# A kernel whose whole instruction order is a table of 4,801 codes: the table searched anew, with the planner's durations rescaled and its margin behind VectorE's reads cut

## The chip, the cores and the metric

One core of a Trainium2 chip. The metric is device time in microseconds (us) of one execution. TensorE is PE in the profile, its weight loads PEld, VectorE DVE, ScalarE ACT, GpSimd POOL, and the engine that issues the DMAs SP.

## The reference, cut to what matters

Two branches over the same 2048 x 512 input `x`, mixed by a gate per row:

```python
# S=2048, D=512, H=32 heads of 16, one shared K and V, F=1792
g = sigmoid((x * gate_w).sum(-1, keepdims=True))
q = (x @ wq).reshape(B, S, H, Dh).transpose(0, 2, 1, 3)
k, v = x @ wk, x @ wv
p = softmax(einsum("bhqd,bkd->bhqk", q, k) * Dh ** -0.5)
a = einsum("bhqk,bkd->bhqd", p, v).transpose(0, 2, 1, 3).reshape(B, S, H * Dh) @ wo
b = (sigmoid(x @ w_gate) * (x @ w_up)) @ w_down
out = g * a + (1 - g) * b
```

## The kernel before

**Tiling.** The attention is cut into 32 units `u` (4 blocks of 512 queries x 8 groups of 4 heads) with 16 key chunks `c` each. A unit first needs the largest score of each query (`maximum`, "m": a matmul at L1148 into a PSUM bank, then a reduction of that bank by VectorE at L1150, 2048 of each). Then come the scores again with the maximum subtracted ("s": a matmul at L1157, then the exponential by ScalarE at L1159, 2048 of each), and after that the product with V (`values`, "V": four 32-column matmuls at L1015, in two passes each, 512 V's in all; each uses the four exponential tiles of one chunk). The feed-forward branch and the output projection are matmuls at L1122 ("f", 4404 of them) that add up in two PSUM banks held for long.

**Two halves.** m, s and f matmuls contract over 64 rows only, so PE runs two at once, one in each half of its rows. One such pair is called a *pair step* here. V fills the whole array. So PE alternates between *stretches* of pair steps and *runs* of V's.

**Banks.** PSUM has 8 banks. An m or s takes a free bank and gives it back when VectorE (m) or ScalarE (s) has read it. A run of V's adds up in one bank. When the run ends, `finish` copies the bank out by ScalarE (L1022), and unless it is the unit's first copy GpSimd adds it to the others (`add_sums`, L1029). A finished f sum is read by ScalarE (`gate` L1131), by VectorE (`gated` L1137), or by `part_of`: the first part of an output tile by ScalarE (L1098), a later one either by VectorE, which adds it to the tile (L1079, "sum"), or by ScalarE into a spare tile (L1098, "apart") that GpSimd then adds (L1101). `gather` chooses between the last two when the program is built, by which would be done first in the plan.

**What sets the order.** `ORDER` is a string. Each code stands for one step of PE: `V` one V, `G` one of 24 opening matmul groups (keys, queries, transposes), `.` a planned wait of 25 units, and a hex digit a pair step whose two base-4 digits say what each half does (1 m, 2 s, 3 f, 0 nothing; so `7` is m beside f, `b` s beside f, `5` m beside m). `State.step` walks the string, keeps a clock in units for each engine, and decides from it which bank is taken, where the readers, the POOL tasks and the DMAs are placed in their engines' queues, and how a part is added. A pair step is 100 units. The rest of the constants are durations in the same units: `RED` a VectorE reduction, `EXP` an exponential, `VALUES` a V, `IN` and `OUT` the change to V's and back, `LATE` from a matmul's start to its reader's, `TAIL` and `FREE` from a reader's end until PE may take the bank again (`FREE_A` behind ScalarE).

```python
    def issue_m(self, h):
        i = self.take()
        ...
        self.free[i] = self.on("dve", self.now + LATE, RED) + TAIL + FREE
```

On the chip there is no clock: every engine executes its own list in order and waits on semaphores. A `.` emits nothing. So if a bank is free sooner than planned PE goes on, and if it is free later PE waits.

Of the kernel before, what the change touches and what calls it, by code (L numbers as in the profile page):

```python
# [31 lines left out]
OU, VB = 2, 2  # L32
# [13 lines left out]
MAX_SPLIT, SQUARE, SEND_SQUARE, PLACE = 180, 75, 220, 320  # L46
EXP, COPY, SCALED = 208, 210, 247
TAIL, TAIL_A = 38, 52

SEEN = 10  # L50


IN, OUT, VALUES = 52, 106, 371

CAST, TWO, CAST_W, TWO_W = 265, 556, 450, 1030


ISSUE, SMALL, TEN_KB, LAST, SAFE, SURE = 185, 750, 20, 300, 300, 150


BEGIN = 2420, 3500, 3200, 2300, 3500, 5250
X1_THERE, WQ_THERE = 5300, (3200, 3450, 4050, 4050)
LATER = (("load_x", 2), 8000), (("load_x", 3), 8100)
FEED_AT = 12200


TURN_OVER, SEEN_OVER = 40, 100
# [55 lines left out]
class State:  # L123

    def __init__(self):
# [3 lines left out]
        self.free, self.sum = [0] * 7 + [4100], None  # L129
# [12 lines left out]
        self.raws, self.raw_free = [], [4700, 6000]  # L142
# [26 lines left out]
    def send(self, n, kb):  # L169

        self.on("sp", self.now, n * ISSUE)
        self.on("dma", self.sp, kb * TEN_KB // 10)
        return max(self.sp + SMALL, self.dma + LAST)

    def issue(self, cost, kb):

        self.on("sp", self.now, cost)
        self.on("dma", self.sp, kb * TEN_KB // 10)
        return max(self.sp + SMALL, self.dma + LAST)
# [39 lines left out]
    def run(self, t):  # L219
# [8 lines left out]
        at = self.on("pool", t[2] if t[2] >= self.ticked else self.ticked + 50, cost)  # L228
# [17 lines left out]
        elif what == "divide":  # L246
            self.divided(args[0], at)
        elif what == "x":
            self.x_done[args[0]] += 1
            if self.x_done[args[0]] == KC // 2:  # L250
                self.x_ready[args[0]] = at + SURE
        elif what == "xf":
            self.x_there[args[0]] = at
        elif what == "max_split":
            self.after(at + 50, "max_square", *args)
        elif what == "wq":

            self.w_there[args[0]] = at if args[0] else at - 500
        else:
            self.ready[args[0]] = at + SURE  # L260
# [33 lines left out]
    def event(self, what, args):  # L294
# [11 lines left out]
        elif what == "place_max":  # L306
            self.max_ready[args[0]] = self.issue(PLACE, 16) + 150
        elif what == "store":
            at = self.sums_free[args[0] % OU] = self.issue(470, 264) + SAFE
            self.after(at, "sums", *args)  # L310
        elif what == "sums":
            self.after(self.issue(430, 136) + 2 * SAFE, "invert", *args)
# [5 lines left out]
        elif what == "spread":  # L318
            u = args[0]
            at = self.issue(250, 128)  # L320
# [108 lines left out]
    def settle(self):  # L429
        for h in range(2):  # L430
            while self.at[h] is not None:
# [13 lines left out]
                elif j.kind == "u":  # L445
# [3 lines left out]
                    self.task(0, at + 50, "h", slot, j.b, 2 * j.i + x)  # L449
# [63 lines left out]
    def issue_m(self, h):  # L513
# [4 lines left out]
        if self.mp[h] == min(self.mp) and self.mp[h] % (2 * NC) == 0:  # L518
            u = self.mp[h] // (2 * NC) - 1
            self.acts.append(("max_finish", u))  # L520
            self.task(0, self.on("dve", 0, ENDS) + 50, "max_split", u)
# [69 lines left out]
    def issue_g(self):  # L591
# [4 lines left out]
        if what == "turn":  # L596
            self.now += 300
            self.ba_release(("v", b), self.now + LATE)
            at = self.on("dve", self.now + LATE - 100, 250)
            self.acts.append(("turned", b, i))  # L600
        else:
            for _ in range(KC):
                self.now += 300
                self.tick()
            at = self.now + LATE - 100
            self.ba_take((what, b, t), 1)
            if what == "keys":
                self.ba_take(("v", b), 1)
                at = self.on("dve", self.on("act", at, 250) + 50, SUM)
                self.ba_release((what, b, t), at)  # L610
                self.k_ready[b] = at + 100
# [5 lines left out]
        self.done += 300 if what == "turn" else 1200  # L617
# [4 lines left out]
    def split_first(self):  # L622
        b = self.next_x
        if b < NB and self.x_loaded[b] <= self.now and (b < 3 or self.first >= GROUPS.index(("turn", 1, 0))):
# [6 lines left out]
            if b == 1:  # L631
                self.x_there[b] = self.on("dve", at - 600, 4 * RED)
# [49 lines left out]
    "fb7ededeef7b7f9f6fbf6fedf75VV59aV692aVV569VV56effedefbdaf7f6bfdb7b7bbdfdbbfd6fef7f7ddd5VVVV7b7bdbedfe7ef6dbfb7ed"
    "ededbf7bb7f6fedebfdfb5VVVVV7b7b79bffbdafdf6fededeedef7e7fb7e7eedff7b5bV95aVVVVV977bfbdef9fb7e7ebdfedeedef7b77bf9"
    "fef6f9ff5eV595VVVVV7b7b7bbdf9fafde7edfedeede7ff6ef7edb7bfefb7aV995VVV565VV7b7b7bbdfeedfedb7fededee7ef7edef97efb7"
    "bbd7bVVV599VVV7b7bb77bbdfbededfedededeef77eef7edbb7fefb75VVVV9edff6edf6fef97bdbfb7b7bbfd6fdefedef7df7775VVV959VV"
    "97b7fbdefbdeb7f9f6fededeef7b7f9faf7b7deff5dVVVVV7b7edbdbf6f9fb7bfededeedef7e7f6f6fef9fb7fb9VVVV969VV6b7bfde7fed6"
    "fede7efbb77bbdfedfedbdb7eeffb75VV596VV596VV997ffbf6f9fbb7dbefdededee7f6ff6f9f7efbff79aVV955VVVV7b7b7b9ff9fbe7edf"
    "edededee7ff6fb76fedefbfb76VV5a9VVVde5eefb7f9fee7dbfbf7ba77fedfedef9bf7bdff755VVVVVdeded6effb7bf9f6fe7b7bb7bfd9ff"
    "ed6fbdeff75dbVVVV65aV6deedffb7b7b7bdbffdde5VV696Vdede6fbf7b7b7bdefbdfd6VVV9b7fde7bfbdbdbb7fedededeef76ffb7bfa7fd"
    "ff5d5VVVVV7b5bbffedb7ee7bdf6fededeedf7bf6faf7f9fff7aaVVV995VVVdee6fdf6fe7bb7fedfb7b7bbdfbd9fef9f6fe7ffd56VVVV6ed"  # L690
    "ededff6fb7be7fbdb7b7bbfdedfb79febdf6fef5VV665VV995VV6deedf7bfb7eedf6fbdb77bb7efdeedfedbf9bf7fb5V695VV956VV95aVV6"
    "7bff9dbf6fef6eddefb7bb7bdfbd7bf6fedefbfedaV695VV695VVVV7b7b7bf9fbdef6.dbdefedeedef7b7ef6fdef6ff7b5a..7V599VV5aaV"
    "V96aVV6eddfef6f6f9fe7bbfdb77bb7efedfed9fbf9b7fdf5VV569VVVV7b7bb7fededeb7f9fe7edededbf7bfe7bb7edbfdfd5VVVV677bbfd"
    "ef6f9feb7bfdededee7fb7ef79fe7bfffd55VVV659VV7b97bfbfded6fbbdf6feeddee7f7bf6fafdf6fbdf5bVVVVV6deef7dbf6fafd7bedfb"
    "7bb7bfdedf9feb7f6bdfef5VV956VVV97bb7b7ffbdedbe7fededeede7fb7fede7bbdf7f7d5VVVVV97fb7bdefb79fbe7efdededee7fb7dbfe"
    "7bdbf6fefaV955VVVVV6dedefe7f6fb7ebdef7b7bb7bdf9ffbdbde7ebfdfd6V695VVVV7b7b7bbdf9fbedf6fedededee7f7ef6f6febdfb7bf"
    "6V959VVVVV6deedef7fe7bedb7dbfb7bb7bdfedefd6fbdbfff575VVV9a6VV696V6ddeeff9f6f9fe7bfbdb7bb7bdff97bfedb7efedef5VV66"
    "9VV559VVV7b7b7bf9fbdeed7efe7ededeef7b7fedef6f9fb7bf9VV569VV6deeeddffb7bf6deb7fb7bb7bdf9ffe7bdeedff7d57VVVVV977bb"
    "7bffbdbedf9fedeeddee7f6ff6f6fbb7efdf76VVV995VVV5b7b7bfefed9fe7bf9fedededef6ff6fb7bfbdeb77dVVV955VVV7b97fbfededed"
    "efefbb7afdfffe7b7b7bf6fedfe5VVVV6dedefe7fe7bbddbfe7b7bb7bdfbdf6fedbe7bdff5dVV659VVV7b7bb7bdf9febd7efededeede7f7e"  # L700
    "bf7bde7bf7fde9VVV5a6VV59aV7b7b7b7bbfdbdeedfedededeef7e7fe7e7bf9fbdf75VVVVVV5eedef7efe79febdfb7b7b7bbfd9fbdfb7bf6"
    "defeddVV655VVV7b7bb7bdfbde7edbdefededee7fe7fe7b7bbddeff76V9a9VV665VV596VV5bbfdeefde76fbdef9f7bb7bbfddbfb7be7f9ee"
    "fedeV659VV695VV56aVV6ddeef7efedb7ebdb7fb7bb77efedfedbdbb7fedf5bV956VV5aaVV96aVVV97bff9e7f6fbf9f97efededeef7b7f9f"
    "6fb7ff7ddd5VVVV7b7bb77bfedbf9defedededeef7b7fe7b7edeef7bf5VV596VV956VV95effef6fedbedf6fb7b7b7bbfdedfbde7ebdbff7d"
    "5VVVV65aV6ddefbf9fe7ef6f9fbdb7b7bbfd7befdbde7efbdd7dVVVVV67bb7bfdf9fbf6edef7ededeef7b7f9faf7dbfe7efbb777VVVVVV9f"
    "dbbdfbe6fdfedededeef76fbf6fdb7efb7f95VV955VVV7b7b97bffedef6dbf9fededeef77e7bf6fef9bbffd5VVVVV7b7b7bb7fedafdedfbd"
    "ededeef7b7fe7e7ef9f9ff76V595VVVVded6fbf6fede7bf97efb7bb7bdff9fb7edeb7dffdd6VV659VVV5e7bfebdfe7edeb7fedbb7b7bbfdf"
# [559 lines left out]
```

## Time and profile before

| | |
|---|---|
| median of 3 runs | 1564.77 us (1564.64 to 1565.0) |
| profiled execution | 1567.49 us, its span 1564.9 us |
| granted PE clock | 1.00 |
| busy share: PE / DVE / ACT / POOL | 99% / 85% / 78% / 51% |
| span up to the first pair step behind the last opening group | 84.4 us |

Read PE's 99% with care. Pair steps overlap two matmuls, and a matmul's record may begin before its weights are loaded, so waits hide inside "busy". The start-to-start spacing of PE's rows is the better measure.

### The profile page before, as it was taken

The numbers are of one execution on the slowest core, as the hardware profiler recorded it, in microseconds if no ns is written. First come the engines' busy times: TensorE is split into PE (matmuls) and PEld (weight loads), VectorE is DVE, ScalarE is ACT, GpSimd is POOL, SyncE is SP. The second block draws the span as 40 slices with busy tenths as digits, with TensorE's granted clock in tenths as the row PEclk, the third lists the DMA queues.
The fourth block names the chain that finished last, engine by engine and source line by source line (L and its number), as shares of the span: only waits on it lengthen the run. The fifth ranks groups of instructions, "written<-read, shape, count | busy, mean of one in ns | idle before, by whom it ended". The sixth has DMA issues, their size and how long they took to land.

```text
span 1564.9 us, 33526 instructions
## 1 busy us (share of the span) xinstructions
PE 1555.2 (99%) x12910; PEld 983.3 (63%) x12910; DVE 1333.5 (85%) x2278; ACT 1228.4 (78%) x2429; POOL 799.4 (51%) x727
## 2 busy tenths in 40 slices
PE   9999999999999999999999999999999999999998
PEld 7766666666656666666655666666665666665653
DVE  6999899988899788889798888898889888888852
ACT  4267778878788787879788787877878878787897
POOL 3353473655584164377475346265658426438351
PEclk9999999999999999999999999999999999999999
DMA  6522120212122121122221212022212212111011
GB/s 233 179 89 57 36 79 24 67 54 89 43 80 65 46 81 53 33 73 63 61 80 54 76 36 87 17 67 67 77 36 91 63 43 80 53 36 56 23 50 48
DMA packets 63219, 103.42 MB, mean 66 GB/s; under 512 B 24546, under 2 KB 25058, under 8 KB 63060
## 3 DMA queue, kind: packets, MB, share of 16 engines
q1 hardware_dynamic: 63060, 101.29, 20.7%
q8 instruction: 101, 1.65, 0.4%
q14 instruction: 58, 0.48, 0.1%
HBM read 79.51 MB, written 21.75 MB: 65 GB/s over the span
## 4 chain that ended last, share of the span: by engine, by line
PE 95%; POOL 2%; DVE 1%; DMA 1%; issue 0%; SPq 0%; ACT 0%; DVEq 0%; POOLq 0%; ACTq 0%
PE bank L1015 29%; PE bank L1122 27%; PE bank L1157 19%; PE bank L1148 17%; PE bank L860 3%; DVE mx L1150 1%; DMA rg<-wg 0%; POOL ou L1029 0%; POOL wu L835 0%; DMA od<-ou 0%; DMA qs<-md 0%; POOL hl L761 0%; PE bank L1203 0%; POOL wg L835 0%; POOL wu L834 0%
## 5 line engine op out<-in xcount | busy, mean ns | idle before, releaser
L1150 DVE TENSOR_REDUCE mx<-bank 128x1 f32<-128x512 f32 x2048 | 1249.1, 681 | 163.9 <-PE bank L1148 102.0
L1159 ACT ACTIVATE p<-bank 128x512 f32<-128x512 f32 x2048 | 1042.2, 690 | 3.6 <-PE bank L1157 1.8
L1157 PE MATMUL bank<-qs,ks 64*128 64x512 f32 x2048 | 727.2, 400 | 0.1
L1148 PE MATMUL bank<-ks,qs 64*128 64x512 f32 x2048 | 682.2, 401 | 0.0
L1015 PE MATMUL bank<-p,v_aug 128*32 128x512 f32 x4096 | 480.1, 597 | 0.0
L1157 PEld LDWEIGHTS bank<-qs,ks 64*128 64x128 f32 x2048 | 359.1, 184 | 127.2 <-ACT p L1159 52.5
L1148 PEld LDWEIGHTS bank<-ks,qs 64*128 64x128 f32 x2048 | 341.9, 185 | 148.7 <-issue 57.2
L1022 ACT COPY ou<-bank 128x512 f32<-128x512 f32 x205 | 126.4, 617 | 268.2 <-PE bank L1015 120.8
L1029 POOL TENSOR_TENSOR ou<-ou,ou 128x512 f32<-128x512 f32 x174 | 222.5, 1279 | 170.5 <-ACT ou L1022 168.1
L1122 PE MATMUL bank<-wd,hl 64*128 64x512 f32 x1344 | 267.5, 382 | 0.0
L1122 PE MATMUL bank<-x,wu 64*128 64x512 f32 x1344 | 266.5, 381 | 0.7 <-SPq L1126 0.7
L1122 PE MATMUL bank<-x,wg 64*128 64x512 f32 x1344 | 265.8, 382 | 0.0
L1015 PEld LDWEIGHTS bank<-p,v_aug 128*32 128x32 f32 x4096 | 113.0, 109 | 242.4 <-issue 214.9
L1122 PEld LDWEIGHTS bank<-wd,hl 64*128 64x128 f32 x1344 | 196.4, 185 | 12.3 <-issue 2.5
L1122 PEld LDWEIGHTS bank<-x,wu 64*128 64x128 f32 x1344 | 196.1, 185 | 9.5 <-issue 2.5
L1122 PEld LDWEIGHTS bank<-x,wg 64*128 64x128 f32 x1344 | 195.6, 185 | 10.0 <-issue 2.0
L1101 POOL TENSOR_TENSOR ba<-ba,pa_d 128x512 f32<-128x512 f32 x35 | 44.3, 1279 | 92.9 <-ACT pa_d L1098 92.8
L834 POOL CAST wg<-rg 128x1024 fp32r<-128x1024 f32 x27 | 28.0, 1038 | 121.7 <-PE bank L1122 56.0
L834 POOL CAST wu<-ru 128x1024 fp32r<-128x1024 f32 x27 | 28.0, 1038 | 94.0 <-PE bank L1122 75.8
L761 POOL TENSOR_TENSOR wd<-rd,wd 128x512 fp32r<-128x512 f32 x56 | 71.6, 1279 | 4.5
L761 POOL TENSOR_TENSOR hl<-h,hl 128x512 fp32r<-128x512 f32 x56 | 71.6, 1279 | 4.5
L1122 PE MATMUL bank<-wa,o 64*128 64x512 f32 x360 | 69.0, 381 | 0.2 <-POOL o L760 0.2
(80 smaller groups left out, 751.2 us busy)
## 6 DMA issues: line engine op xcount, KB each, us to landing
rg<-wg SPq DMA_DIRECT2D x28, 512.0 KB
ru<-wu SPq DMA_DIRECT2D x28, 512.0 KB
rd<-wd SPq DMA_DIRECT2D x28, 512.0 KB
qs<-qd SPq DMA_DIRECT2D x192, 64.0 KB
qd<-q SPq DMA_DIRECT2D x32, 256.0 KB
od<-ou SPq DMA_DIRECT2D x31, 256.0 KB
xf<-x_in SPq DMA_DIRECT2D x16, 256.0 KB
vd<-od SPq DMA_DIRECT2D x32, 128.0 KB
```

The source lines that it names most:

```text
L761: lo.tensor_tensor(hl[:, 1, :], raw, f32(hl[:, 0, :]), op=ALU.subtract)
L834: nc.gpsimd.tensor_copy(WS[item][:, 0, :], raw)
L860: nc.tensor.matmul(to, w[:, p, part(kc)], x, start=i == 0, stop=i == 3 * KC - 1)
L1015: nc.tensor.matmul(ps[32 * j:32 * j + 32, :], v_aug[:, c, :], PT.pop((u, c, j)), start=start, stop=stop)
L1022: nc.scalar.copy(to, ps)
L1029: nc.gpsimd.tensor_tensor(SUMS[u], SUMS[u], PARTS_OF[u].pop(0), op=ALU.add)
L1101: nc.gpsimd.tensor_tensor(BA[b, t], BA[b, t], PA[b, t].pop(0), op=ALU.add)
L1122: ins = nc.tensor.matmul(pairs(banks[i]), l, turns(r), start=start, stop=stop)
L1148: nc.tensor.matmul(pairs(banks[i]), qs_t[u % 3][r, pr, part(qt)], turns(ks[r, kb * 512:(kb + 1) * 512]), start=True, stop=True)
L1150: nc.vector.tensor_reduce(MX[u][:, pr, h, qt, kb:kb + 1], banks[i], axis=AX.X, op=ALU.max)
L1157: nc.tensor.matmul(pairs(banks[i]), ks[r, part(c)], turns(qs_t[u % 3][r, pr, :]), start=True, stop=True)
L1159: nc.scalar.activation(p, banks[i], AF.Exp, scale=0.25)
```

## The change

The durations are rescaled by 1.066 (`RED` 260 to 277, `EXP` 208 to 222, the DMA and POOL costs likewise), with the pair step staying at 100 units. Against a VectorE reduction a pair step is thus planned 6% shorter. `OUT` falls from 106 to 92 units and `FREE` from 65 to 35. A query group costs 1264 in place of 1200. `ORDER` is a new string for these figures. No instruction changes its work; only positions, banks and the choice of `gather` change. After the change every line number is one higher.

```diff
-LATE, LATE_A, FREE, FREE_A = 190, 200, 65, 60
+LATE, LATE_A, FREE, FREE_A = 197, 207, 35, 60
-RED, GATED, SUM, ENDS, INVERSE, LOWER = 260, 258, 285, 115, 70, 285
+RED, GATED, SUM, ENDS, INVERSE, LOWER = 277, 275, 304, 123, 75, 304
-EXP, COPY, SCALED = 208, 210, 247
-TAIL, TAIL_A = 38, 52
+EXP, COPY, SCALED = 222, 222, 264
+TAIL, TAIL_A = 40, 55
-IN, OUT, VALUES = 52, 106, 371
+IN, OUT, VALUES = 55, 92, 398
-CAST, TWO, CAST_W, TWO_W = 265, 556, 450, 1030
+CAST, TWO, CAST_W, TWO_W = 282, 593, 480, 1098
...
             for _ in range(KC):
-                self.now += 300
+                self.now += 300 if what == "keys" else 316
...
 ORDER = (
-    "GGGGGGG555G55G555G55........5GG55G555GG555GG77777Gffdfdffffddddddfffffffff7775.5..GG555GG555G55G9efef7ee7edf6f9f"
+    "GGGGGGG.....555G455G515G..5454G545GGG555GG55Gdd5dG57fffffffff77577ffffffffffdd15GG555GdddddGddd5G57.7Gab7fef77fb"
```

Counted in the two strings and in the actions that they produce. A *long* stretch has 14 pair steps or more between two runs of V's, a *short* one fewer (nearly all three):

| behind the last opening group | before | after |
|---|---|---|
| pair steps | 4190 | 4201 |
| of these with one half empty | 2 | 36 |
| V's, and the runs they form | 512 in 196 | 512 in 243 |
| planned waits `.` | 3 | 108 |
| long stretches, their pair steps | 95, 3871 | 93, 3700 |
| short stretches, their pair steps | 101, 319 | 150, 501 |
| m and s in the long stretches | 1626 and 1788 | 1473 and 1634 |
| other VectorE reads ended there: `gated`, "sum" | 56, 19 | 53, 56 |
| other ScalarE reads there: `gate`, L1098 parts, `finish` | 54, 61, 85 | 53, 18, 89 |

Ahead of it the opening has 61 pair steps, 13 blocks of G's and 11 waits before, and 70, 14 and 8 now. In the whole program `finish` copies and POOL's `add_sums` go from 205 and 174 to 262 and 231, parts added by VectorE from 23 to 65, and parts taken apart by ScalarE and added by POOL from 45 to 3.

**Place 1, TensorE**, chunks 10 and 11 of unit 9. `p_10_0_1` is an exponential tile of chunk 10, `v_aug` holds V, `ks` and `qs` are keys and queries. Before, the chunks lie inside one run of five V's, and a long stretch follows:

```order
L1015 MATMUL bank_72<-p_10_1_0_6909,v_aug 32x512
L1015 MATMUL bank_72<-p_10_1_1_6891,v_aug 32x512
L1015 MATMUL bank_72<-p_11_0_0_6966,v_aug 32x512
L1015 MATMUL bank_72<-p_11_0_1_6951,v_aug 32x512
L1015 MATMUL bank_72<-p_11_1_0_6935,v_aug 32x512
L1015 MATMUL bank_72<-p_11_1_1_6930,v_aug 32x512
L1148 MATMUL bank_75<-ks,qs_109 128x512
L1122 MATMUL bank_79<-x_0_4306,wu_2_5932 128x512
```

Chunk 10 and chunk 11 add up in one bank, with nothing between them. On the same engine at the same two chunks now:

```order
L1016 MATMUL bank_75<-p_10_1_0_6916,v_aug 32x512
L1016 MATMUL bank_75<-p_10_1_1_6919,v_aug 32x512
L1158 MATMUL bank_72<-qs_107,ks 128x512
L1149 MATMUL bank_76<-ks,qs_109 128x512
L1149 MATMUL bank_78<-ks,qs_109 128x512
L1158 MATMUL bank_74<-qs_107,ks 128x512
L1149 MATMUL bank_79<-ks,qs_109 128x512
L1149 MATMUL bank_73<-ks,qs_109 128x512
L1016 MATMUL bank_77<-p_11_0_0_6972,v_aug 32x512
L1016 MATMUL bank_77<-p_11_0_1_6982,v_aug 32x512
```

Three pair steps (two s and four m, no f) moved in between the chunks; they came out of the long stretches. Chunk 11 begins a new run in another bank.

**Place 2, ScalarE and VectorE**, the second down-projection part of the first block's output tiles 0 and 1 (`ba`). Before, ScalarE scales both sums out of their banks between two exponentials:

```order
L1159 ACTIVATE p_5_0_1_3007<-bank_75 128x512
L1159 ACTIVATE p_6_0_0_3017<-bank_77 128x512
L1098 ACTIVATE pa_0_d_3025<-bank_72,gom 128x512
L1098 ACTIVATE pa_1_d_3036<-bank_73,gom 128x512
L1022 COPY ou_3059<-bank_76 128x512
```

`pa_0` and `pa_1` are spare tiles, which POOL adds to `ba` later. Now VectorE adds the two banks to the tiles itself, between two reductions:

```order
L1151 TENSOR_REDUCE mx_2176<-bank_76 128x1
L1151 TENSOR_REDUCE mx_2176<-bank_79 128x1
L1080 SCALAR_TENSOR_TENSOR ba_0_1838<-bank_73,gom,ba_0_1838 128x512
L1080 SCALAR_TENSOR_TENSOR ba_1_1852<-bank_78,gom,ba_1_1852 128x512
L1151 TENSOR_REDUCE mx_2176<-bank_72 128x1
L1151 TENSOR_REDUCE mx_2176<-bank_79 128x1
```

Two reads moved from ScalarE's list to VectorE's, and two additions left POOL's.

More of the change, by code (lines that the diff above doesn't have):

```diff
@@ L127, in __init__ @@
         self.full = True
-        self.free, self.sum = [0] * 7 + [4100], None
+        self.free, self.sum = [0] * 7 + [4370], None
         self.later, self.count = [], 0
@@ L254, in run @@
         elif what == "max_split":
-            self.after(at + 50, "max_square", *args)
+            self.after(at + 53, "max_square", *args)
         elif what == "wq":
-            self.w_there[args[0]] = at if args[0] else at - 500
+            self.w_there[args[0]] = at if args[0] else at - 533
         else:
@@ L319, in event @@
             u = args[0]
-            at = self.issue(250, 128)
+            at = self.issue(266, 128)
             if u % 2 or u == NU - 2:
@@ L616, in issue_g @@
             self.acts.append((what + "_out", b, t, i))
-        self.done += 300 if what == "turn" else 1200
+        self.done += {"turn": 320, "keys": 1200, "query": 1264}[what]
         self.free[i] = at + TAIL_A + FREE
```

129 lines of the change are left out of this document (65 added, 64 removed).

## The prediction

> **What bounds the kernel now.** I read the page's busy shares first, then the groups of instructions, then PE's rows in order of time around the two chunks of place 1, then the two readers' rows in the same window.
>
> ```profile
> PE 1555.2 (99%) x12910; PEld 983.3 (63%) x12910; DVE 1333.5 (85%) x2278; ACT 1228.4 (78%) x2429; POOL 799.4 (51%) x727
> PE 95%; POOL 2%; DVE 1%; DMA 1%; issue 0%; SPq 0%; ACT 0%; DVEq 0%; POOLq 0%; ACTq 0%
> L1150 DVE TENSOR_REDUCE mx<-bank 128x1 f32<-128x512 f32 x2048 | 1249.1, 681 | 163.9 <-PE bank L1148 102.0
> L1157 PEld LDWEIGHTS bank<-qs,ks 64*128 64x128 f32 x2048 | 359.1, 184 | 127.2 <-ACT p L1159 52.5
> L1148 PEld LDWEIGHTS bank<-ks,qs 64*128 64x128 f32 x2048 | 341.9, 185 | 148.7 <-issue 57.2
> ```
>
> PE carries 95% of the chain that ends last. Its weight loads nevertheless stand idle in front of m and s, partly until ScalarE has read a bank. PE's rows (start, length, line, count) show what a step costs when nothing is late:
>
> ```profile
> 539.05 1.07 PE L1015 MATMUL bank<-p,v_aug 128*32 128x512 f32 x8
> 540.05 0.48 PE L1148 MATMUL bank<-ks,qs 64*128 64x512 f32 x2
> 540.37 0.38 PE L1157 MATMUL bank<-qs,ks 64*128 64x512 f32 x1
> 540.90 4.50 PE L1015 MATMUL bank<-p,v_aug 128*32 128x512 f32 x40
> 545.33 0.48 PE L1148 MATMUL bank<-ks,qs 64*128 64x512 f32 x1
> 545.65 0.38 PE L1157 MATMUL bank<-qs,ks 64*128 64x512 f32 x1
> 545.86 0.38 PE L1148 MATMUL bank<-ks,qs 64*128 64x512 f32 x1
> 546.08 0.38 PE L1157 MATMUL bank<-qs,ks 64*128 64x512 f32 x1
> 546.94 0.38 PE L1148 MATMUL bank<-ks,qs 64*128 64x512 f32 x1
> 547.16 0.38 PE L1122 MATMUL bank<-x,wu 64*128 64x512 f32 x2
> 555.45 1.07 PE L1015 MATMUL bank<-p,v_aug 128*32 128x512 f32 x8
> ```
>
> - *Pair step*: from 545.65 to 547.16 there are seven, 0.2158 us each.
> - *V*: one V took 1.00 (539.05 to 540.05), five took 4.43 (540.90 to 545.33). So a V is 0.858, and leaving a run costs 0.14 once.
> - *Run*: the second pair behind a run comes after 0.32, 0.105 over a step. The three steps of the short stretch from 540.05 to 540.90 fill 0.85, so the change to V's costs another 0.85 - 0.647 - 0.105 = 0.095. A run costs 0.34 in all, whatever its length.
> - *Long stretch*: 545.33 to 555.45 is 10.12 us. It holds 43 steps (the string's piece behind that run), 9.28, and 0.20 for its two ends. That leaves 0.64 us of stall, and the short stretch has none.
>
> Now the whole phase behind the opening. These rows give its begin and its end (1551.74 + 3.19 = 1554.93), with the span 1564.9:
>
> ```profile
> 84.39 0.48 PE L1157 MATMUL bank<-qs,ks 64*128 64x512 f32 x1
> 1551.74 3.19 PE L1015 MATMUL bank<-p,v_aug 128*32 128x512 f32 x28
> ```
>
> It lasts 1470.5 us. By price: 4190 steps x 0.2158 = 904.2, 512 V's x 0.858 = 439.3, 196 runs x 0.34 = 66.6, together 1410.1. So 60.4 us are stalls. The short stretches, at 0.014 each (a mean of my own over the 97 of three steps, from their first and last rows), have 1.4 of that. The 95 long ones have 0.62 us each, as in the example.
>
> Who causes them? Both readers, in the same window:
>
> ```profile
> 545.91 9.06 DVE L1150 TENSOR_REDUCE mx<-bank 128x1 f32<-128x512 f32 x15 [2.26 <-PE bank L1148]
> 554.89 0.68 DVE L1137 SCALAR_TENSOR_TENSOR h<-gs,bank 128x512 f32<-128x512 f32 x1
> 545.52 0.59 ACT L1022 COPY ou<-bank 128x512 f32<-128x512 f32 x1 [3.82 <-PE bank L1015]
> 546.06 10.40 ACT L1159 ACTIVATE p<-bank 128x512 f32<-128x512 f32 x21
> 550.63 0.18 PEld L1148 LDWEIGHTS bank<-ks,qs 64*128 64x128 f32 x1 [0.15 <-ACT p L1159]
> ```
>
> VectorE ran 15 reductions in one piece, 0.599 from start to start ((9.06 - 0.68) / 14). ScalarE ran 21 exponentials in one piece, 0.485 apart ((10.40 - 0.69) / 20). Both are full over the whole long stretch and idle during V's (2.26 and 3.82). The weight load at 550.63 waits for an exponential that had stood in ScalarE's queue. So in the long stretches the readers set the pace, PE runs ahead of them until the banks are out, and then waits. In the runs of V's PE alone sets it.
>
> **The change part by part.** *Steps, V's, runs.* Steps 4201 x 0.2158 = 906.6, V's 439.3, 243 runs x 0.34 = 82.6: 1428.5, or 18.4 more than before without stalls. Of this 16.0 are the 47 more runs and 2.4 the 11 steps that half-empty pairs add. All of it lies on PE and so on the path. The exits cost what they do because a matmul waits for its weights:
>
> ```profile
> 540.05 0.19 PEld L1148 LDWEIGHTS bank<-ks,qs 64*128 64x128 f32 x2 [0.84 <-ACT ba L1098]
> 540.16 0.19 PEld L1157 LDWEIGHTS bank<-qs,ks 64*128 64x128 f32 x1
> ```
>
> The second pair's load starts at 540.16 and its matmul at 540.37, when the load of 0.19 is over; behind a run no load had gone ahead. [...]
>
> *Readers' work moved.* This is the main gain. Before, a long stretch gives VectorE (1626 x 0.599 + 56 x 0.60 + 19 x 0.66) / 95 = 10.74 us of work and ScalarE (1788 x 0.485 + 54 x 0.48 + 61 x 0.52 + 85 x 0.48) / 95 = 10.17. The prices of the smaller reads are estimates, their rows' durations less the 0.08 (DVE) or 0.2 to 0.3 (ACT) by which neighbours overlap:
>
> ```profile
> L1137 DVE SCALAR_TENSOR_TENSOR h<-gs,bank 128x512 f32<-128x512 f32 x56 | 36.7, 675 | 0.0
> L1079 DVE SCALAR_TENSOR_TENSOR ba<-bank,gom,ba 128x512 f32<-128x512 f32 x13 | 9.6, 741 | 0.0
> L1131 ACT ACTIVATE gs<-bank 128x512 f32<-128x512 f32 x56 | 36.8, 763 | 5.1 <-PE bank L1122 4.9
> L1098 ACT ACTIVATE pa_d<-bank,gom 128x512 f32<-128x512 f32 x35 | 26.6, 836 | 0.0
> L1022 ACT COPY ou<-bank 128x512 f32<-128x512 f32 x205 | 126.4, 617 | 268.2 <-PE bank L1015 120.8
> L1029 POOL TENSOR_TENSOR ou<-ou,ou 128x512 f32<-128x512 f32 x174 | 222.5, 1279 | 170.5 <-ACT ou L1022 168.1
> ```
>
> PE's own steps take 3871 x 0.2158 / 95 = 8.79 there, 9.41 with the stall. VectorE thus ends 1.33 behind PE's stretch and ScalarE 0.76. Afterwards the same sums give VectorE 951 / 93 = 10.23, ScalarE 870 / 93 = 9.36 and PE 3700 x 0.2158 / 93 = 8.585. The reads lost per stretch (0.51 and 0.81) now run under the short stretches and V's around them. A short cycle of two V's and three steps lasts 1.72 + 0.34 + 0.65 = 2.7 us and holds 3.3 reductions (2.0 us) and 2.8 exponentials with a copy (1.8), so it has room.
>
> *What stall remains.* Lower end: the 107 planned waits in the long stretches, which are 25 units or 0.054 us each, 5.8 us or 0.062 a stretch. Upper end: VectorE may end no further behind PE than before, so the stretch must last 10.23 - 1.33 = 8.90, a stall of 0.315, 29.3 us in all; by ScalarE it would be 9.36 - 0.76 - 8.585 = 0.015. I take the lower end, for it comes from the reads' placing stretch by stretch, and add the cut of the margin once per stretch. `FREE` was 65 units of 2.30 ns (0.599 / 260), 0.150 us, and is 35 of 2.16, 0.076; the reads themselves are no faster, so PE meets the missing 0.074. That makes 0.136 x 93 = 12.6, and 150 short stretches x 0.014 = 2.1: 14.7 us.
>
> *The work around it.* 57 more copies take ScalarE 27 us, while 42 parts fewer free 22; POOL gets 57 additions and loses 42, 15 x 1.279 = 19 us. The 42 sums are 28 us for VectorE. That is POOL at 53% and VectorE at 88% of the new span, inside the sums above; the V's hide POOL's part, and if that cover went a copy would find its spare tile taken and the V's bank would stay out. SP issues the same DMAs. I cost this at nothing. The opening has nine steps and one block more (2.2) and three waits fewer. Between 0 and 2.2 I take 1.1, so 85.5. The tail of 10.0 (1554.93 to 1564.9) is untouched.
>
> Sum: 85.5 + 1428.5 + 14.7 + 10.0 = 1538.7 against a span of 1564.9. That profiled execution is given as 1567.49, the runs' median 1564.77 lies at the span, so I forecast 1539 for the median.
>
> **Rivals.** *VectorE stays the bound of the long stretches.* Its share rises, and its 15 reductions in one piece speak for it; that it ends behind PE by an amount the order sets, not the chip, speaks against. It gives the upper end: 1524.0 + 29.3 + 2.1 = 1555.
>
> *Slower: the cut margin makes as many weight loads late as now.* A load that finds its bank unread starts late, and its step with it, as behind the exits. Readers that are less full speak against, and so does the three-step stretch without a stall. For it speaks that the plan now counts on a bank 0.074 earlier at every reduction. If the stalls stay at 60.4, the time is 1524.0 + 60.4 = 1584. It decides from 40.8 us on, 0.44 a long stretch (1564.8 - 1524.0).
>
> *A wash.* With a stall of 0.41 to 0.47 a stretch, what the runs add eats what the readers give back: 1565.
>
> **How the numbers follow.** My forecast (1525 to 1547) has 0.62: below it stand 1524 with no stall, above it 0.24 a stretch. VectorE's bound (1547 to 1560) has 0.24, the wash 0.05, the slower case 0.09. The range 1525 to 1560 holds the first two, 0.86. Differences under 0.2%, 3 us, can't be told from none, so faster 0.86, same 0.05, slower 0.09.
>
> **What would show it.** Right: PE's rows in the long stretches at 0.216 with about 0.14 of stall a stretch, the idle time of weight loads in front of m and s smaller per run, and reductions no longer in one piece from end to end. Wrong first step: runs that cost more than 0.34. Wrong second step: VectorE in one piece through the long stretches, with PE's loads waiting for it rather than for ScalarE. The forecast fails if short stretches, now 150, stall too: 0.1 in each would be 15 us.

## The result, and the profile after

| | before | after |
|---|---|---|
| median of 4 runs each, same chip | 1564.7 us (1564.27 to 1565.0) | 1548.35 us (1547.4 to 1550.06) |
| ratio | | 0.9897 [0.988, 0.9914] |
| profiled execution, its span | 1567.49, 1564.9 | 1548.13, 1546.4 |
| stalls behind the opening | 60.2 us | 23.4 us |

The kernel is 1.0% faster, 16 us; the forecast was 26. These lines of the page of the changed kernel answer to those shown of before (all line numbers are one higher; `PEclk` is PE's granted clock in tenths, in 40 equal slices of the span):

```profile
PE 1529.7 (99%) x12910; PEld 974.6 (63%) x12910; DVE 1363.8 (88%) x2320; ACT 1236.7 (80%) x2444; POOL 820.4 (53%) x742
PEclk9999999999999999999999999999999999999998
PE 96%; POOL 1%; DMA 1%; DVE 1%; SPq 0%; ACT 0%; issue 0%; DVEq 0%; POOLq 0%
L1151 DVE TENSOR_REDUCE mx<-bank 128x1 f32<-128x512 f32 x2048 | 1255.3, 680 | 100.6 <-PE bank L1149 57.2
L1149 PEld LDWEIGHTS bank<-ks,qs 64*128 64x128 f32 x2048 | 330.4, 185 | 141.9 <-ACT p L1160 50.5
L1158 PEld LDWEIGHTS bank<-qs,ks 64*128 64x128 f32 x2048 | 343.0, 185 | 115.6 <-ACT p L1160 31.7
```

VectorE is busier in a shorter span, and the idle time in front of its reductions fell by 63 us. That in front of the weight loads of m and s fell by only 18 us in all, while PE's stalls fell by 37. A load that stands behind a run, like the one at 540.05 shown with the prediction, counts its 0.8 us as idle too, and there are 47 more runs; per run the two groups fell from 1.41 to 1.06. At the same two chunks PE's rows (start, length, line, count) now read:

```profile
541.54 1.92 PE L1016 MATMUL bank<-p,v_aug 128*32 128x512 f32 x16
543.40 0.70 PE L1158 MATMUL bank<-qs,ks 64*128 64x512 f32 x3
...
544.24 1.92 PE L1016 MATMUL bank<-p,v_aug 128*32 128x512 f32 x16
546.10 0.48 PE L1149 MATMUL bank<-ks,qs 64*128 64x512 f32 x2
...
555.25 1.06 PE L1016 MATMUL bank<-p,v_aug 128*32 128x512 f32 x8
```

A run of two V's takes 1.86, three pair steps 0.84, and the next run again 1.86: the short stretch has no stall. The long one lasts from 546.10 to 555.25, 9.15 us for 41 steps (8.85) and its ends (0.20), so 0.10 of stall in place of 0.64. The readers in the same window:

```profile
544.77 0.68 DVE L1151 TENSOR_REDUCE mx<-bank 128x1 f32<-128x512 f32 x1
546.61 7.86 DVE L1151 TENSOR_REDUCE mx<-bank 128x1 f32<-128x512 f32 x13 [1.16 <-PE bank L1149]
554.40 0.67 DVE L1138 SCALAR_TENSOR_TENSOR h<-gs,bank 128x512 f32<-128x512 f32 x1
546.28 0.59 ACT L1023 COPY ou<-bank 128x512 f32<-128x512 f32 x1
546.83 8.93 ACT L1160 ACTIVATE p<-bank 128x512 f32<-128x512 f32 x18
```

Both are still full from end to end, with fewer reads: 13 reductions where there were 15, 18 exponentials where there were 21. The reads of the short stretch lie ahead of these rows. So the stall fell together with the readers' work in a long stretch, as forecast; that the reductions would no longer come in one piece did not show. What this does not explain stands in one place near the end. These rows give a stretch of time, its length, the busy time of PE, PEld, DVE, ACT and POOL (with instructions), PE's granted clock, the DMA share and GB/s:

```profile
1510.00:1513.00 3.00, 3.00 (x30) 2.30 (x32) 0.71 (x2) 2.68 (x6) 0.00 (x0) 1.00 0.16 43
1513.00:1516.40 3.40, 1.25 (x9) 0.18 (x1) 0.72 (x2) 1.88 (x4) 0.00 (x0) 1.00 0.25 95
1516.40:1526.70 10.30, 6.58 (x26) 3.09 (x28) 2.16 (x3) 2.77 (x5) 3.14 (x3) 0.50 0.03 9
1526.70:1536.30 9.60, 9.60 (x81) 3.15 (x81) 0.75 (x1) 8.05 (x16) 0.00 (x0) 1.00 0.00 0
```

PE stands still, and then runs at half clock for 10.3 us. The rows of the same place, in order of time on each engine:

```profile
1513.77 0.48 PE L1158 MATMUL bank<-qs,ks 64*128 64x512 f32 x1
1519.99 0.79 PE L1123 MATMUL bank<-we,o 64*128 64x512 f32 x1 [5.75 <-POOL o L761]
...
1504.64 1.59 DVE L1080 SCALAR_TENSOR_TENSOR ba<-bank,gsig,ba 128x512 f32<-128x512 f32 x2 [14.48 <-PE bank L1123]
1506.15 0.24 DVE L1053 RECIPROCAL rc<-rc 128x16 f32<-128x16 f32 x1
...
1501.14 0.34 SPq L1044 DMA_DIRECT2D rc<-sd  x1
1508.16 0.32 SPq L1057 DMA_DIRECT2D rd<-rc  x1
1511.69 0.51 SPq L1065 DMA_DIRECT2D vd<-od  x1
...
1518.01 1.26 POOL L1071 TENSOR_TENSOR vd<-vd,bc 128x512 f32<-128x512 f32 x1 [16.73 <-DMA vd<-od]
1519.33 0.61 POOL L761 CAST o<-vd 128x512 fp32r<-128x512 f32 x1
```

This is how the softmax of the last unit but one (30) is divided out. Its sums go to DRAM and come back (`rc`), VectorE takes the reciprocal, which goes to DRAM and comes back spread over the rows (`bc`) with the unnormalized output (`vd`). POOL multiplies and makes `o`, and the projection of it (f with weights `we`) can begin. The reciprocal stood in VectorE's list behind two additions to `ba`, which waited for PE. Its store was issued only 1.8 us after it, behind SP's waits for PE (5.9 us at L1127). So the chain took 18.8 us from the issue of `rc` to the end of the cast. PE met the projection at once behind a V: of the first pair step the s went at 1513.77, and the projection's matmul beside it waited 5.75 us. The standstill is 6.0 us, and 6.7 us of the work after it ran at half clock (pair steps 0.43 apart, 1523.63 to 1524.06, where the price is 0.2158), 3.4 more by an estimate from the clock of 0.50: 9.4.

The same chain in before, its first issue, POOL's two instructions and PE's first step of the projection:

```profile
1528.32 0.91 SPq L1043 DMA_DIRECT2D rc<-sd  x1
...
1541.22 1.27 POOL L1070 TENSOR_TENSOR vd<-vd,bc 128x512 f32<-128x512 f32 x1 [14.68 <-DMA vd<-od]
1542.56 0.61 POOL L760 CAST o<-vd 128x512 fp32r<-128x512 f32 x1
...
1544.33 0.91 PE L1122 MATMUL bank<-we,o 64*128 64x512 f32 x5
```

The cast was done at 1543.17, 14.9 us behind the issue, and PE came 1.2 us later. `State.step` takes each code of the string without a question. The rule for the projection stands in `State.has`, which this kernel never calls: the division must have been emitted and the weights be there; when `o` is done is not asked. The string searched anew put the two next to each other, and the plan itself says so: walked through without the chip, it has the first projection step at 694413 units, while POOL's division runs until 695650, 12 pair steps later. In the plan of before the step comes 8.5 pair steps behind the end of the division.

### The profile page after: what moved, and what is told of

Read it like the earlier page. It is cut to its first block, busy times and chain, and to the rows that moved or that the text cites. A ratio compares the mean times of both kernels' runs of the same rounds, so it can differ in the third digit from the quotient of the medians.

```text
span 1546.4 us, 33600 instructions
## 1 busy us (share of the span) xinstructions
PE 1529.7 (99%) x12910; PEld 974.6 (63%) x12910; DVE 1363.8 (88%) x2320; ACT 1236.7 (80%) x2444; POOL 820.4 (53%) x742
## 4 chain that ended last, share of the span: by engine, by line
PE 96%; POOL 1%; DMA 1%; DVE 1%; SPq 0%; ACT 0%; issue 0%; DVEq 0%; POOLq 0%
PE bank L1123 31%; PE bank L1016 30%; PE bank L1149 16%; PE bank L1158 16%; PE bank L861 2%; DVE mx L1151 0%; DMA vd<-od 0%; DMA rx<-x_in 0%; SPq L976 0%; POOL hl L762 0%; PE bank L1204 0%; POOL wg L836 0%; POOL wu L836 0%; DMA qs<-qd 0%; POOL ou L1030 0%
## 5 line engine op out<-in xcount | busy, mean ns | idle before, releaser
L1160 ACT ACTIVATE p<-bank 128x512 f32<-128x512 f32 x2048 | 1040.7, 645 | 12.6 <-PE bank L1158 8.8
L1158 PE MATMUL bank<-qs,ks 64*128 64x512 f32 x2048 | 671.2, 392 | 0.0
L1149 PE MATMUL bank<-ks,qs 64*128 64x512 f32 x2048 | 642.5, 395 | 0.3 <-DMA qs<-qd 0.3
L1030 POOL TENSOR_TENSOR ou<-ou,ou 128x512 f32<-128x512 f32 x231 | 295.5, 1280 | 323.5 <-ACT ou L1023 319.7
L1023 ACT COPY ou<-bank 128x512 f32<-128x512 f32 x262 | 156.5, 598 | 232.1 <-PE bank L1016 138.7
L1123 PE MATMUL bank<-x,wg 64*128 64x512 f32 x1344 | 246.6, 377 | 1.4 <-SPq L1127 1.4
L1123 PE MATMUL bank<-x,wu 64*128 64x512 f32 x1344 | 245.9, 377 | 0.0
L1123 PE MATMUL bank<-wd,hl 64*128 64x512 f32 x1344 | 245.4, 378 | 0.0
L836 POOL TENSOR_TENSOR wg<-rg,wg 128x1024 fp32r<-128x1024 f32 x28 | 66.5, 2376 | 5.9 <-ACT wg L826 3.8
L761 POOL CAST hl<-h 128x512 fp32r<-128x512 f32 x56 | 34.3, 612 | 65.9 <-DVE h L1138 65.7
L836 POOL TENSOR_TENSOR wu<-ru,wu 128x1024 fp32r<-128x1024 f32 x28 | 66.5, 2374 | 2.2
```

The lines of the kernel that those rows point to most:

```text
L761: hi(hl[:, 0, :], raw)
L836: nc.gpsimd.tensor_tensor(WS[item][:, 1, :], raw, f32(WS[item][:, 0, :]), op=ALU.subtract)
L1023: nc.scalar.copy(to, ps)
L1030: nc.gpsimd.tensor_tensor(SUMS[u], SUMS[u], PARTS_OF[u].pop(0), op=ALU.add)
L1123: ins = nc.tensor.matmul(pairs(banks[i]), l, turns(r), start=start, stop=stop)
L1149: nc.tensor.matmul(pairs(banks[i]), qs_t[u % 3][r, pr, part(qt)], turns(ks[r, kb * 512:(kb + 1) * 512]), start=True, stop=True)
```

## The experiments

Every stall below is reckoned as in the prediction: the phase behind the opening less steps, V's and runs at their three prices. Only the end is set 0.2 us earlier, at the price of the last V and not at the end of its row, so before has 60.2 here and 60.4 there. Where a stall is put down to a reader, it was counted step by step, by the bank that PE waited for and which engine had to read it. These counts are a reckoning and no line of a view, and they don't add up to the whole; take them as rough.

**The hole at the end.** The first edit brings the projection later, the second the division earlier. *late_e* puts the work of the last 27 codes of `ORDER` in another order, with the halves paired otherwise and nine planned waits more, and leaves the other codes alone. (Each line shows the end of the string, behind its first three dots; all other dots are planned waits. By the new plan one part of an output tile goes back from VectorE to ScalarE and POOL.)

```diff
-    ...bbbVbbfeffe3aVeaaVVaaaVVaa2VVVV
+    ...bbbVaaaVVaaaVVaa....aVVeaef....ff.3f3VVV
```

> The changed kernel with the last 27 codes of its order in another sequence: the projection steps that need the last unit pair (line 1123, from the tile o) come behind nine more exponential pairs and five more V's, about 8 us later on PE; the same work in all. Theory (the missed term): in the changed kernel PE stood still from 1513.8 to 1520.0 for o and then ran at half the clock until 1526.7, about 9.5 us in all. Then the span falls from 1546.4 to 1537, the time to about 1539 (ratio 0.983 to 0.985), the clock is 1.00 until the tail. Rival: at this place ScalarE is the bound anyway (20 exponentials x 0.485 = 9.7 us follow each other), so PE waits for it instead and at most 4 us are won (1544). Second rival: the clock falls at the end for another reason than the stand-still; then 6 us are won and the half clock stays in the trace (1542).

Measured: 1539.82 us (1539.44 to 1540.14), ratio to before 0.9839 [0.9825, 0.9852], span 1538.2, granted clock 1.000, stalls 14.8. The projection begins at 1523.04 and does not wait, although the cast is 2.2 us later than in the changed kernel:

```profile
1521.18 1.92 PE L1017 MATMUL bank<-p,v_aug 128*32 128x512 f32 x16
1523.04 0.48 PE L1124 MATMUL bank<-we,o 64*128 64x512 f32 x1
...
1521.49 0.61 POOL L762 CAST o<-vd 128x512 fp32r<-128x512 f32 x1
```

So the hole cost 8.5 us of the median, and both rivals named beforehand (1544, 1542) are out. *early_inv* leaves `ORDER` as it is and emits unit 30's reciprocal, its store and its spreading right behind the sums:

```diff
-    for what, *args in plan():
+    todo = plan()
+    chain = [next(a for a in todo if a[0] == what and a[1] == NU - 2) for what in ("invert", "send_inverse", "spread")]
+    todo = [a for a in todo if all(a is not c for c in chain)]
+    at = next(n for n, a in enumerate(todo) if a[0] == "sums" and a[1] == NU - 2) + 1
+    todo[at:at] = chain
+    for what, *args in todo:
```

> The changed kernel with three steps of unit 30 emitted earlier: its reciprocal on VectorE and the two groups of DMAs behind it on SP stand right behind the load of the sums, ahead of two VectorE adds and of SP's waits between halves. Nothing else moves. Theory: the reciprocal stood behind two adds in VectorE's list (1504.6 to 1506.2) and its store behind SP's waits until 1508.2, so the chain to o starts 4.4 us earlier, PE's stand-still falls from 6.2 to 1.5 to 2 us, and if a stand-still of that length doesn't lower the clock, the half clock goes too: the span falls by 7.5 to 8.5, to 1538 to 1539. If it does lower the clock: by 4 to 5, to 1542. Rival: the chain is set by the landing of its DMAs (the last took 6.2 us), which do not come sooner because they wait for one another: under 1 us won, 1546.

Measured: 1540.88 us (1540.72 to 1542.16), ratio 0.9847 [0.9834, 0.9861], span 1538.9, clock 1.000. The rows that answer to those of the hole:

```profile
1503.03 0.25 DVE L1053 RECIPROCAL rc<-rc 128x16 f32<-128x16 f32 x1 [12.64 <-DMA rc<-sd]
...
1503.31 0.32 SPq L1057 DMA_DIRECT2D rd<-rc  x1
...
1512.89 1.29 POOL L1071 TENSOR_TENSOR vd<-vd,bc 128x512 f32<-128x512 f32 x1 [11.47 <-DMA vd<-od]
...
1514.91 0.48 PE L1123 MATMUL bank<-we,o 64*128 64x512 f32 x1 [0.43 <-POOL o L761]
1516.26 0.48 PE L1123 MATMUL bank<-we,o 64*128 64x512 f32 x2 [0.65 <-POOL o L762]
```

The store goes out 4.85 us earlier, and of the 5.75 us of waiting 0.43 and 0.65 are left. Both edits, from opposite ends of the chain, give back nearly the same, 7.5 and 8.5 us: the cause is shown.

**Which reader set the stalls before.** Three kernels are the kernel before with lighter reads: *b_halfred* leaves half of the columns out of the maxima, *b_halfexp* half of the exponentials (V reads the half that is there twice), *b_halfboth* does both. Each ran once; the spans are those of the profiled execution.

```diff
-        nc.vector.tensor_reduce(MX[u][:, pr, h, qt, kb:kb + 1], banks[i], axis=AX.X, op=ALU.max)
+        nc.vector.tensor_reduce(MX[u][:, pr, h, qt, kb:kb + 1], banks[i][:, :256], axis=AX.X, op=ALU.max)
```

```diff
-            nc.tensor.matmul(ps[32 * j:32 * j + 32, :], v_aug[:, c, :], PT.pop((u, c, j)), start=start, stop=stop)
+            nc.tensor.matmul(ps[32 * j:32 * j + 32, :].rearrange("p (a n) -> p a n", a=2), v_aug[:, c, :],
+                             PT.pop((u, c, j))[:, :256].unsqueeze(1).to_broadcast([P, 2, 256]), start=start, stop=stop)
...
-        nc.scalar.activation(p, banks[i], AF.Exp, scale=0.25)
+        nc.scalar.activation(p[:, :256], banks[i][:, :256], AF.Exp, scale=0.25)
```

> The kernel before with VectorE's reductions over 256 of the 512 columns (the maxima leave out half of the scores); PE and ScalarE have the same work. Theory A: the 15.0 us of stall behind reductions go, and what stood behind exponentials stays, 43 to 50 us: span 1550 to 1556. Theory B (VectorE binds alone): the stall falls to what ScalarE asks for, (10.17 - 0.76) against 9.41, that is hardly at all: 1560 to 1565. Rival C (PE's own): 1565.

> The kernel before with ScalarE's exponentials over 256 of the 512 columns; V reads these columns twice, so PE's work is the same (the other half of the probabilities is left out). ScalarE's 2048 exponentials take about half as long. Stalls before: 60.2 us in the phase behind the opening. Theory A (waits counted by the queue that PE waited for: 43.5 us behind exponentials, 15.0 behind reductions): 15 to 30 us of stall remain and the span is 1520 to 1535. Theory B, that of the prediction's second case (VectorE ends 1.33 us behind PE in every long stretch and would bind alone, 10.74 - 1.33 = 9.41 us a stretch): the stall stays near 60 and the span near 1565. Rival C (the stalls are PE's own, weight loads and semaphores): no change, 1565.

> The kernel before with both readers lightened: reductions and exponentials over 256 of 512 columns (half of the scores left out of maxima and probabilities), PE's list the same. Theory: all stalls of the phase behind the opening are waits for the two readers' queues; 60.2 us fall to 2 or less and the span to 1503 to 1507. Rival: part of the stall is PE's own (weight loads that start late, semaphores, the waits between halves on SP); then 10 to 40 us remain, 1513 to 1545.

| | span | stalls | a long stretch | put down to |
|---|---|---|---|---|
| before | 1564.9 | 60.2 | 0.623 | ScalarE 43.5, VectorE 15.0 |
| reductions halved | 1560.3 | 57.8 | 0.598 | ScalarE 55.5 |
| exponentials halved | 1543.6 | 40.1 | 0.406 | VectorE 29.8 |
| both halved | 1506.1 | 3.7 | 0.046 | |

Some of the waits of PE's weight loads point the same way (us in all, times, the longest). First before, then with halved reductions, then with halved exponentials:

```profile
PEld bank L1157 <- ACT p L1159: 52.5, 192, 0.8
PEld bank L1148 <- DVE mx L1150: 8.9, 23, 0.8
```

```profile
PEld bank L1157 <- ACT p L1159: 68.2, 265, 0.8
```

```profile
PEld bank L1158 <- DVE mx L1151: 34.2, 148, 0.8
```

Nearly all stalls were the two readers' lists, since all but 3.7 us go when both are lighter. ScalarE was the first bound: without VectorE's load 57.8 of the 60.2 us stay. VectorE stood close behind and would have held 40.1 by itself. Halving one alone buys 2 or 20 us, halving both 56. Either alone buys less than expected: by theory A, which went by the counts, 43 to 50 us should have stayed in the first kernel and 15 to 30 in the second. The first came out in the range of theory B, the second between the two. Which engine a wait is put down to does not say what comes back when that engine is faster.

**The additions moved from ScalarE and POOL to VectorE.** *b_sum* does this one part of the change in the kernel before: 42 of its 45 parts taken apart are added by VectorE, at the old places.

```diff
+    todo, moved = [], {}
+    for a in plan():
+        if a[0] == "part" and a[4] == "apart" and sum(moved.values()) < 42:
+            moved[a[1].b, a[2]] = moved.get((a[1].b, a[2]), 0) + 1
+            todo.append(("part", *a[1:4], "sum"))
+        else:
+            todo.append(a)
+    for key, n in moved.items():
+        for _ in range(n):
+            todo.remove(next(a for a in todo if a[0] == "add" and a[2:] == key))
```

> One part of the change alone, in the kernel before: 42 of the 45 parts that ScalarE took out of their banks and POOL added are added by VectorE, at the same places of the lists; the order of PE is the same. Theory by the lightened runs: VectorE gets 0.29 us more a long stretch and would need 11.03 - 1.54 = 9.49 against 9.41 now, ScalarE would need 9.16: VectorE becomes the first bound, the stall grows by about 7 us, 1570 to 1573 (ratio 1.003 to 1.006). Rival: ScalarE is the bound in nearly all stretches and 22 us less of it count: 1545 to 1555 (ratio 0.988 to 0.994).

Measured: 1572.71 us (1571.43 to 1573.4), ratio 1.0043 [1.0028, 1.0057]. The size is as expected, the place is not. The long stretches rose by 1.1 us only (0.623 to 0.635 each), the short ones by 5.3 (1.5 to 6.8). Behind VectorE 20.6 us were counted, 15.0 in before. By itself, in the old order, this part loses.

*l_apart* undoes it in *late_e*: 42 of 46 down-projection parts go back to ScalarE and POOL, each addition right behind its part. *l_apart12* sends back every fourth, 11 in all (the second diff shows the lines that differ).

```diff
-    for what, *args in plan():
+    todo, moved = [], 0
+    for a in plan():
+        if a[0] == "part" and a[4] == "sum" and a[1].kind == "d" and moved < 42:
+            moved += 1
+            todo += [("part", *a[1:4], "apart"), ("add", None, a[1].b, a[2])]
+        else:
+            todo.append(a)
+    for what, *args in todo:
```

```diff
+        if a[0] == "part" and a[4] == "sum" and a[1].kind == "d":
+            seen += 1
+        if a[0] == "part" and a[4] == "sum" and a[1].kind == "d" and seen % 4 == 0:
```

> The changed kernel with the later projection, and one part of the change undone: 42 of the 46 down-projection parts that VectorE adds are scaled out by ScalarE and added by POOL again, at the same places of the lists. From the lightened runs: VectorE may end 1.53 behind PE and ScalarE 0.74. VectorE then has 9.93 us a long stretch (needs 8.40, under PE's 8.585), ScalarE 9.60 (needs 8.86): stall 0.275 x 93 = 25 us against 14.8, span 1546 to 1551 (time 1548 to 1553, ratio 0.989 to 0.992). Rival: VectorE is what PE waits for now (12.6 us counted against 6.1), so taking 28 us off it gains: span 1530 to 1535.

> As l_apart with only every fourth down-projection part (11) moved back, spread over the program. By the same sums VectorE needs 8.62 a long stretch (stall 0.035), ScalarE 8.68 (0.095), against 0.12 and 0.08 without it: within 2 us of the later projection alone, span 1536 to 1540, time 1538 to 1542 (ratio 0.983 to 0.986). Rival: the balance matters stretch by stretch and VectorE's worst stretches are helped: 3 to 5 us faster, 1533 to 1535.

Measured: *l_apart* 1557.32 us (1555.79 to 1560.53), ratio 0.9954 [0.994, 0.9968], 17.5 over *late_e* and beyond what was expected. *l_apart12* 1542.2 us (1541.42 to 1542.53), ratio 0.9855 [0.984, 0.9869], 2.4 over it where at most 2 were expected. In *l_apart* the long stretches hold 31.1 us of stall against 14.8. The middle one rose from 0.136 to 0.179 only; most of the rest are six new holes of 1.2 to 4.3 us. The page, then the waits between 370 and 381 us, then those between 736 and 746, then a stretch of time near the largest hole:

```profile
PE 1539.4 (99%) x12910; PEld 979.9 (63%) x12910; DVE 1340.0 (86%) x2277; ACT 1260.8 (81%) x2487; POOL 872.8 (56%) x785
```

```profile
ACT ou L1024 <- POOL ou L1031: 2.2, 1, 2.2
PEld bank L1159 <- ACT ou L1024: 2.2, 1, 2.2
```

```profile
PEld bank L1124 <- SPq L1128: 1.9, 1, 1.9
SPq L755 <- POOL wd L763: 2.5, 1, 2.5
```

```profile
754.30:757.70 3.40, 3.40 (x19) 3.15 (x18) 1.84 (x3) 1.91 (x4) 1.82 (x1) 0.50 0.36 111
```

POOL is busy 56%, yet at 370 a spare tile is given back 2.2 us late: ScalarE's copy waits for it, and the exponentials behind the copy, and PE's load, wait too. At 736 SP waits 2.5 us for POOL's split of a weight tile, and behind that stands the wait at L1128 by which one half's matmuls follow the other's. At 747 and 1112 SP waits 8.9 and 5.5 us for such a split (the first is over at 751.48, and SP issues the next load at 751.51), with the same wait behind it. Half clock comes on top at 754.3 and at 375.4. So four of the six holes, 13.9 us, are POOL's list and not the two readers'. In the new order, taking the move to VectorE back costs 17.5 us; in the old order the move alone loses, as *b_sum* shows. The expectation had the balance of VectorE and ScalarE in view and missed POOL. One thing stays open: no search placed the additions that went back to POOL, and with one made for them less might be lost.

**What is left.** *l_halfred* and *l_halfexp* are *late_e* with the lighter reads of above.

> The changed kernel with the later projection (span 1538.2, stall 14.8 us in the long stretches), reductions over 256 of 512 columns. Worked out from the two lightened runs of the kernel before: ScalarE alone asked for 9.39 us a long stretch there with 10.17 of work, so it may end 0.78 behind PE; now it has 9.36, so 8.58 against PE's 8.585: 0 to 3 us of stall remain, span 1524 to 1527. Rival: stalls behind exponentials (6.1 us counted) stay or grow, since PE comes sooner: 8 to 12 us, 1531 to 1535.

> The changed kernel with the later projection, exponentials over 256 of 512 columns, reductions whole. VectorE alone asked for 9.20 us a long stretch before with 10.74 of work, so it may end 1.54 behind PE; now it has 10.23, so 8.69 against 8.585: 0.105 x 93 = 9.8 us of stall remain and the span is 1532 to 1535. Rival: the two readers wait on each other through the shared banks, and without ScalarE's queue VectorE's waits go too: under 4 us, 1526.

Measured: reductions halved, span 1533.1, stalls 10.2, so the rival's branch. Two holes behind SP (1.96 at 314, 1.28 at 1409) hold 3.2 of it. Exponentials halved, span 1537.8, 3 over the expected range, with 15.2 of stall for 9.8 expected. One hole holds 3.9 of that, and the other 92 long stretches have 0.133 each, behind VectorE. That hole is 2 us in *late_e*, at the same place and with another cause than a reader. The waits of *late_e* between 316 and 326 us, and SP's rows:

```profile
PEld bank L1124 <- SPq L1128: 1.7, 1, 1.7
```

```profile
319.85 1.23 SPq L977 DMA_DIRECT2D qs<-qd  x3
322.53 0.23 SPq L979 DMA_DIRECT2D qs<-zeros  x1
```

L1128 is the wait between the halves again. It stands in SP's list behind the DMAs that load a set of queries (`load_q(7)`), which SP issues one after another. *late_q* moves that load behind the two waits:

```diff
-    for what, *args in plan():
+    todo = plan()
+    q7 = next(a for a in todo if a[0] == "load_q" and a[1] == 7)
+    todo.remove(q7)
+    at = next(n for n, a in enumerate(todo) if a[0] == "f" and a[1] == 1 and a[2].key == ("g", 0, 6) and a[4] == a[2].n - 1)
+    todo.insert(at + 1, q7)
+    for what, *args in todo:
```

> The changed kernel with the later projection, and the load of unit 7's queries (eight DMA issues on SP) emitted behind the two waits between halves of gate tile 6 that stood behind it in SP's list; nothing else moves. Theory: PE's 1.8 us at 321.0 to 322.9 were SP's list, where the wait between the halves came last: they go, the span falls from 1538.2 to 1536.4, the time to 1538 (ratio 0.983). Rival: unit 7's queries come too late then, or SP's list only moves the same wait to a weight load: no change, 1538.

Measured: **1537.84 us** (1537.1 to 1538.33), ratio to before 0.9827 [0.9812, 0.9842], span 1536.0, stalls 12.7, 0.138 a long stretch. This beats both kernels.

## Why the prediction was right or wrong

| term of the sum, us | forecast | changed kernel | late_e |
|---|---|---|---|
| opening | 85.5 | 84.3 | 84.9 |
| steps, V's, runs | 1428.5 | 1428.5 | 1428.5 |
| stalls in 93 long stretches | 12.6 | 14.4 | 14.8 |
| stalls in 150 short stretches | 2.1 | 8.7 | 0.5 |
| half clock in a V, ends of the phase | | 0.3 | -0.6 |
| tail | 10.0 | 10.1 | 10.1 |
| span | 1538.7 | 1546.4 | 1538.2 |

The steps, V's and runs stand at their price in all three columns; the rows of stalls and the one below them are what each trace has over it.

- *Steps, V's and runs*: right. In *late_e* all V's and the leaving of their runs are together 0.4 us off their price, so 47 more runs cost what a run cost before. The second pair behind a run still comes 0.32 after the first (543.40 to 543.72 in the changed kernel), and in *late_e* the third behind the run at 1523.04 comes after 0.53 (at 1523.57), two steps and 0.10. Inside a stretch a matmul's record can begin before its load is over: in before a load lasts from 550.84 to 551.02 and its matmul's record begins at 550.95.
- *Long stretches*: right in size, 0.136 forecast and 0.155 to 0.160 found, 0.138 once the hole at 321 us is closed. Whether the two parts of it (0.062 of planned waits, 0.074 for the cut margin) are the real ones was not shown: the margin acts only through a search of the order, and no kernel with the old margin and a new search was run. The bullet on VectorE has another source for the same size, so that the figure was met is in part luck. That the reads moved to the short stretches are what relieved the long ones fits the sums and the rows; no run changed the number of short stretches alone.
- *Short stretches*: they do not stall, 0.003 each in *late_e* against 0.014. What the changed kernel has there is the hole.
- *The step that failed* is the work around the stretches: "SP issues the same DMAs. I cost this at nothing." The DMAs were the same, but their place against PE was not. The chain through VectorE's reciprocal, SP's stores and POOL's cast had 1.2 us to spare before and came 6 us late after. The prediction looked at the readers of the banks only, never at the last chain of DMAs, for which POOL's row in before, 14.68 us idle behind `vd<-od`, would have been the place. The smaller hole at 321 us is the same step in small.
- *The median at the span*: 2 us short. The four runs of the changed kernel lie 1.7 to 2.9 above their spans; before's own profiled execution also lies 2.6 above, and took 2.7 longer than the median.
- *VectorE as the bound*, the rival at 1555. The measured 1548.35 lies in the interval that the prediction gave this rival (1547 to 1560) and just outside that of its own forecast (1525 to 1547). That is chance: the hole brought it there, and without the hole *late_e* is at 1539.82. The rival is refuted in its time, for a reason that the prediction had wrong. Its allowance, that VectorE ends 1.33 behind PE, was read off a trace in which ScalarE set the stall. With light exponentials VectorE alone asks 8.79 + 0.41 = 9.20 a stretch, so it can end 10.74 - 9.20 = 1.54 behind. With 1.54 the same sum gives 10.23 - 1.54 - 8.585 = 0.105 after, and *l_halfexp* has 0.133, nearly all of the 0.138 that *late_q* has left. So VectorE's end was 1536 (1524.0 + 93 x 0.105 + 2.1) and not 1555: VectorE does set most of what remains, but at the size that the forecast had from other reasons. The sign that the prediction named for this rival did show: the reductions come in one piece, and by the count in *late_e* PE waits more for VectorE than for ScalarE (12.6 us against 6.1). That sign does not tell 0.1 of stall from 0.3. For ScalarE *b_halfred* gives 0.78 where the prediction had 0.76; its sum is then nothing, and *l_halfred* has 0.08 a stretch beside its two holes. No kernel with both reads halved was run in the new order.
- *Slower, or a wash*: the loads behind the cut margin are not late at large; the long stretches fell from 59.2 us to 14.4.

## What to carry to other kernels

When an order of work is changed to relieve the engines that bound it, look up also the longest chain of small DMAs that crosses it, and compare how long it took from its first issue to its last cast with the distance that the new order leaves it. Where a planner keeps clocks, ask it first: this one had the projection ahead of its input on paper. An engine's allowance to run late is read only from a run in which that engine, and not its neighbour, sets the stall: lighten the other one and read again. An engine at 56% can be the bound for 2 us at a time, and whoever waits in order behind it turns that into a stall of the engine at 99%.

## What the runs showed of the hardware

A pause can cost more than its length: that of 6.0 us in the changed kernel cost 9.4 with the half clock behind it, by the estimate given with its rows. The clock fell to 0.50 there at 1516.4, 2.6 us behind the start of PE's last matmul, and stayed so for 10.24 us, of which 6.7 fell on work. Shorter pauses gave shorter stretches: about 3.4 us in *l_apart* behind 754.3 (0.50 over the 3.40 us of the row shown above; the pause was 2.16, 751.69 to 753.85), as much at 375.4, where matmul rows of 0.63 in place of 0.38 stand up to 378.6, and again in *l_halfexp*; 10.24 is about three times that. This row of *l_halfexp* lies behind its hole:

```profile
323.20:326.70 3.50, 3.50 (x20) 2.81 (x18) 2.40 (x5) 1.84 (x5) 0.00 (x0) 0.51 0.43 150
```

PE's matmuls stand 2.06 us apart there (319.92 to 321.98), and at the same hole 1.85 in *late_e* (321.02 to 322.87), where the clock stayed at 1.00. So about 2 us of pause, with matmuls on both sides, can bring half clock or not. What decides it was not shown: no run moved a pause to see.
